# Retention and a two-layer MLP on one core: no key-value products for the last chunk of a batch, and a new order of all work

## The chip, the cores and the metric

The kernel runs on one core of a Trainium2 chip. The time is device microseconds of one execution; the median of several runs is compared. A core has five instruction queues: PE (TensorE, matmuls; its weight loads are listed as PEld), DVE (VectorE), ACT (ScalarE), POOL (GpSimd) and SP (SyncE, DMA issues only). Each works strictly in its own order and waits on semaphores for the others. Matmul results go to PSUM, everything else lies in SBUF.

## The reference, cut to what matters

```
scores = q @ k^T / 8                             # 8 batches, 8 heads, 576 tokens, 64 per head
D[i, j] = gamma_h ** (i - j)  if i >= j else 0
ret = (scores * D) @ v
x = ret as (4608 tokens, 512)                    # heads side by side
h = x @ w_in                                     # 512 -> 2048
g = max(0.01 * h, h)
out = g @ w_out                                  # 2048 -> 512
```

All inputs and the output are float32; the kernel multiplies in float16 and adds up in float32.

## The kernel before, in words

**Retention.** The 576 tokens of a batch are nine chunks of 64. Two chunks in a row, over all eight heads, are a *unit* of 128 tokens: 36 units, u = 0 to 35, chunk numbers 2u and 2u + 1 (j = 0, 1). `CB` is 9, so `(2*u + j) % CB` is the chunk's place in its batch. For each unit q, k and v are loaded in float32 (`ld`u.0, .1, .2 for q, k, v; line 865), cast to float16, q and v with the decay factors (`cq`, `ck`, `cv`, lines 892 to 900: one instruction on VectorE or GpSimd, but eight, one a head, for a scaling on ScalarE), and q and k are turned, by TensorE for units 0 to 7 (`tp`, line 938, and the copy back `yt`, 945) and by a DMA transpose for two units at a time from unit 8 on (`tr`, 921). Then come matmuls of 64x64: scores within the chunk (`sa`, line 973), the key-value product k^T v (`sb`, line 982), masking on VectorE (`mk`, 988), the running state in float32 (`st`, 1031 to 1038) and its float16 copy (`sx`, 1051 and 1054). The output product (line 1096) adds masked scores times v and state times q. These small matmuls come in groups: `oa` (all of a unit's output), `ca` and `ow` (scores with state products, then the unit's own products) and, from unit 13 on, one burst `bu` for everything. The result is copied to xT, turned as layer 1 wants it (`x`u, 1145).

**The MLP.** Tokens go in nine groups of 512, four units each. Layer 1 of groups 0 to 2 is done plainly (`h`group.column.token, line 1201, and the activation `l`, 1208): sixteen matmuls with 128 columns for group 0, eight with 256 for the others. Groups 3 to 8 do layer 1 (`a`, line 1382), and all groups layer 2 (`b`, line 1465), by Winograd's form of Strassen's method: seven half-size products p1 to p7 instead of eight, with sums of weights (`ws`, `wm`), of inputs (`xs`, `m`) and of accumulators, which are copied or added on ScalarE and VectorE (`cA`, `u2`, `k5`, and the four outputs `11`, `12`, `21`, `22`). Four PSUM accumulators (tile acc) are shared by `tp`, `h`, the fillers and the products. Results go out by `so` (line 1293). The weights are loaded by GpSimd's queue: `wi0` to `wi3` are quarters of w_in, `wo0` to `wo3` of w_out.

**What sets the order.** A planner (class `Plan`) gets every job with its engine, an estimated cost, the jobs it comes after, its buffers and a due time. It places the jobs one by one on a model of the five engines and of the DMA queues, the most urgent first, and the program is written in that order. Three tables in `_cfg` steer it: `eng` says which engine does a job where it is not the default, `nudge` shifts the urgency of named jobs, `shift_due` the due times of sets of products. Where the planner sees TensorE waiting early on, it puts in matmuls on a tile of zeros, the fillers (`filler`, line 1574, tile idle):

```
early = t < CFG["fill_tight"]
if t - free < (350 if early else 500) or t > CFG["fill_until"]:
    return None
```

The planner's costs do not run on the chip; only the order, the engines and the number of fillers that follow from them do.

Of the kernel before, what the change touches and what calls it, by code (L numbers as in the profile page):

```python
# [47 lines left out]
class Plan:  # L48
# [72 lines left out]
    def order(self, margin=30, slack=30, filler=None):  # L121
# [57 lines left out]
        while todo:  # L179
# [76 lines left out]
def _cfg():  # L256
# [40 lines left out]
    nudge = {  # L297
        -125060:
            "b1.p2.1 ",
        -12876:  # L300
            "so3.1 ",
        -129001:
            "b1.p4.1 ",
        -135715:
            "b1.21 ",
        -137832:
            "b1.11 ",
        -149466:
            "b2.p4.1 ",
        -1547:  # L310
            "mk25 ",
        -15631:
            "b3.p5.0 ",
        -15982:
            "mk27 ",
        -166028:
            "m3.3.0 ",
        -168918:
            "tp5.1 ",
        -18270:  # L320
            "a7.0.p7.0 ",
        -19132:
            "bu32 ",
        -224663:
            "wm1.1 ",
        -2292:
            "m5.2.1 ",
        -239388:
            "wm0.1 ",
        -23999:  # L330
            "b4.p6.1 ",
        -241662:
            "ws3.1 ",
        -25911:
            "ck33 ",
        -2823:
            "b3.p7.1 ",
        -283444:
            "h1.8.256 ",
        -284183:  # L340
            "b0.11 ",
        -289278:
            "ws3.0 ",
        -291604:
            "h1.10.256 ",
        -292799:
            "h1.4.256 ",
        -292880:
            "h1.14.256 ",
        -293315:  # L350
            "b1.p1.1 ",
        -295060:
            "h2.12.0 ",
        -296205:
            "m0.2.0 ",
        -296904:
            "h1.0.0 ",
        -296915:
            "h1.2.0 ",
        -297398:  # L360
            "wm3.1 ",
        -298104:
            "h1.6.0 ",
        -298106:
            "h1.4.0 ",
        -298370:
            "h1.2.256 ",
        -298539:
            "m0.0.1 ",
        -299439:  # L370
            "tp3.1 ",
        -303300:
            "h2.14.0 ",
        -308278:
            "h1.8.0 ",
        -308311:
            "h1.0.256 ",
        -308822:
            "b1.p1.0 ",
        -309432:  # L380
            "h0.12.256 ",
        -311524:
            "h1.6.256 ",
        -311811:
            "h2.10.0 ",
        -311836:
            "h1.12.256 ",
        -313357:
            "h0.12.384 ",
        -313360:  # L390
            "h0.12.128 ",
        -335793:
            "h0.8.384 ",
        -34182:
            "m5.1.0 ",
        -35130:
            "x32 ",
        -354662:
            "b0.p1.1 ",
        -3566:  # L400
            "h2.8.256 ",
        -357776:
            "h0.4.384 ",
        -367256:
            "b0.p2.1 ",
        -373798:
            "b0.p4.1 ",
        -373977:
            "b0.p2.0 ",
        -37443:  # L410
            "m2.3.1 ",
        -37836:
            "b5.p5.0 ",
        -37837:
            "m5.2.0 ",
        -411099:
            "h0.0.384 ",
        -412537:
            "b1.p2.0 ",
        -42785:  # L420
            "so1.0 ",
        -42873:
            "b6.p6.1 ",
        -43046:
            "b6.cA ",
        -44602:
            "b6.p3.0 ",
        -475499:
            "sb5 ",
        -476800:  # L430
            "tp5.0 ",
        -477521:
            "ow4 ",
        -48742:
            "b7.cA ",
        -5032:
            "bu25 ",
        -5392:
            "st13.1 ",
        -60255:  # L440
            "a8.3.p7.0 ",
        -6102:
            "h2.8.0 ",
        -6129:
            "st22.1 ",
        -6251:
            "h2.10.256 ",
        -6440:
            "st5.1 ",
        -67999:  # L450
            "h2.0.0 ",
        -6861:
            "x13 ",
        -6863:
            "mk15 ",
        -69572:
            "sb6 ",
        -7013:
            "st16.1 ",
        -71217:  # L460
            "ow8 ",
        -741035:
            "h0.8.128 ",
        -7443:
            "bu16 ",
        -78873:
            "sb9 ",
        -79153:
            "ca8 ",
        -7916:  # L470
            "ck31 ",
        -80887:
            "b8.p1.1 ",
        -80940:
            "ow9 ",
        -8500:
            "h2.12.256 ",
        -86291:
            "h2.4.0 ",
        -86992:  # L480
            "ca6 ",
        -87129:
            "ca9 ",
        -88867:
            "h2.6.0 ",
        -91309:
            "ca10 ",
        -9164:
            "h2.14.256 ",
        -93902:  # L490
            "h2.4.256 ",
        -94450:
            "xs4.0 ",
        -94496:
            "cq18 ",
        -949:
            "mk23 ",
        -95343:
            "ck19 ",
        -95691:  # L500
            "sb10 ",
        -97722:
            "h2.6.256 ",
        10483:
            "cq5 ",
        121673:
            "mk3 ",
        132759:
            "b1.u2 ",
        14115:  # L510
            "sx4 ",
        16903:
            "b2.u2 ",
        18328:
            "ck21 ",
        19089:
            "a8.0.p3.0 ",
        20427:
            "cv23 ",
        206971:  # L520
            "h2.2.256 ",
        21595:
            "x28 ",
        221749:
            "h2.2.0 ",
        2247:
            "a5.0.p5.0 ",
        22662:
            "cv9 ",
        24175:  # L530
            "a4.2.p5.0 ",
        24632:
            "x16 ",
        24762:
            "xs4.2 ",
        26177:
            "cq9 ",
        262811:
            "st3.1 ",
        27608:  # L540
            "a5.0.p7.0 ",
        28146:
            "mk18 ",
        28610:
            "a5.0.p3.0 ",
        28749:
            "cq23 ",
        29413:
            "st24.0 ",
        305690:  # L550
            "tr10 ",
        3073:
            "bu27 ",
        30779:
            "a5.0.p2.0 ",
        319187:
            "tr8 ",
        34356:
            "b5.p7.1 ",
        3442:  # L560
            "bu28 ",
        34544:
            "xs5.2 ",
        3603:
            "b4.p5.1 ",
        3689:
            "b1.p6.0 ",
        38799:
            "x29 ",
        4280:  # L570
            "b7.p5.0 ",
        46305:
            "a7.2.p2.0 ",
        4876:
            "b1.p6.1 ",
        54112:
            "b5.p4.0 ",
        5838:
            "b6.p1.1 ",
# [127 lines left out]


CFG = _cfg()


# [972 lines left out]
```

## Time and profile before

| | |
|---|---|
| median of 3 runs | 288.48 us (288.45 to 289.79) |
| the profiled execution | 286.13 us |
| its span, first to last instruction | 284.1 us |
| granted TensorE clock, mean | 0.999 |
| TensorE busy | 274.5 us, 97% |
| VectorE, ScalarE, GpSimd busy | 78%, 64%, 33% |
| HBM read and written | 36.81 MB, 9.44 MB |

The profile is one execution. Its page gives busy times, the span in 40 slices (tenths of busy time, TensorE's clock and the DMA's share), the DMA queues, and the chain of work that ended last. The views of the trace that are used below are groups of instructions by line, the timeline (start, length, engine, line, operation, tiles, count; in brackets the idle time before it and what ended it), and windows (start and end, length, then for each engine busy time and count, TensorE's clock, DMA share and GB/s). "issue" as a releaser means that nothing in the profile accounts for the wait.

### The profile page before, as it was taken

What the parts mean: (1) busy time and instruction counts of PE and PEld (TensorE: products, weight loads), DVE (VectorE), ACT (ScalarE), POOL (GpSimd) and SP (SyncE); (2) the same over time, 40 slices, a digit from 0 to 9 for tenths busy, and PEclk for the clock granted to TensorE, in tenths of its full rate; (3) what the DMA queues carried; (4) which work ended last, traced back from release to release, by engine and by line L of the source; (5) the groups of instructions that cost most, each with busy time, mean ns of one, the idle gap of its engine ahead of it and who ended that gap; (6) DMA issues with size and microseconds to landing.
All of it is one profiled execution on the core that took longest, in us unless ns stands there. A gap on an engine that the chain in (4) does not pass through costs nothing.

```text
span 284.1 us, 10441 instructions
## 1 busy us (share of the span) xinstructions
PE 274.5 (97%) x4530; PEld 231.8 (82%) x4530; DVE 221.9 (78%) x394; ACT 182.2 (64%) x373; POOL 92.9 (33%) x109
## 2 busy tenths in 40 slices
PE   8989899999999999999999999999999999999994
PEld 3668787887788888888888878888888888888883
DVE  3775899865888699898969889889897876955762
ACT  2366576676579598768767766877656755755720
POOL 8888987910122311337324134522100000000000
PEclk9999999999999999999999999999999999999999
DMA  7999999999999999999999999990312002100304
GB/s 158 290 262 237 275 183 284 320 217 228 273 234 194 226 231 272 202 225 240 225 224 212 230 215 229 248 229 0 76 47 105 2 2 76 75 0 3 148 2 148
DMA packets 118797, 50.06 MB, mean 176 GB/s; under 512 B 107488, under 2 KB 112224, under 8 KB 118752
## 3 DMA queue, kind: packets, MB, share of 16 engines
q1 hardware_dynamic: 110368, 35.82, 55.6%
q0 software_dynamic: 7056, 13.11, 19.2%
q8 instruction: 35, 0.57, 0.8%
q10 hardware_dynamic: 1328, 0.47, 0.6%
q14 instruction: 10, 0.08, 0.1%
HBM read 36.81 MB, written 9.44 MB: 163 GB/s over the span
## 4 chain that ended last, share of the span: by engine, by line
PE 82%; DVE 7%; DMA 5%; issue 2%; POOL 2%; ACT 0%; DVEq 0%; POOLq 0%; ACTq 0%
PE acc L1465 38%; PE acc L1382 26%; PE acc L1201 10%; PE ot L1096 4%; DMA w_in<-in_moe_w_in_dram 3%; DMA qkT<-qk 2%; PE sc L982 2%; PE sc L973 2%; POOL t L865 1%; DVE mix L1441 1%; DVE sum L1409 1%; PE acc L938 1%; DVE v L896 1%; DVE s L1037 1%; DVE s L988 1%
## 5 line engine op out<-in xcount | busy, mean ns | idle before, releaser
L1465 PEld LDWEIGHTS <-gt 128*128 128x128 f16 x720 | 69.6, 98 | 8.9 <-ACT gt L1405 0.3
L1465 PE MATMUL acc<-w_out,gt 128*128 128x256 f16 x432 | 54.4, 273 | 0.1
L1201 PE MATMUL acc<-xT,w_in 128*128 128x128 f16 (+1 forms) x512 | 47.1, 246 | 0.5 <-issue 0.5
L1201 PEld LDWEIGHTS <-w_in 128*128 128x128 f16 x512 | 39.1, 98 | 4.4 <-issue 0.7
L1382 PEld LDWEIGHTS <-w_in 128*128 128x128 f16 x384 | 36.8, 98 | 5.5 <-issue 0.8
L1414 ACT ACTIVATE gt<-sum 128x512 f16<-128x512 f32 x48 | 29.8, 629 | 17.8 <-DVE sum L1409 17.7
L1208 ACT ACTIVATE gt<-acc 128x512 f16<-128x512 f32 x48 | 27.8, 594 | 19.9 <-PE acc L1201 19.7
L1405 ACT ACTIVATE gt<-acc 128x512 f16<-128x512 f32 x48 | 28.6, 595 | 14.5 <-PE acc L1382 14.0
L896 POOL TENSOR_TENSOR qk<-t,cs 128x512 f16<-128x512 f32 x19 | 20.6, 1090 | 50.7 <-PE sc L982 22.1
L1465 PE MATMUL acc<-w_mix,gt 128*128 128x256 f16 x288 | 36.4, 273 | 0.0
L1465 PEld LDWEIGHTS <-mix 128*128 128x128 f16 x288 | 27.7, 98 | 4.0 <-DVE mix L1441 0.5
L1382 PEld LDWEIGHTS <-w_sum 128*128 128x128 f16 x288 | 27.6, 98 | 3.9 <-DVE xs L1362 0.4
L1382 PE MATMUL acc<-xs,w_in 128*128 128x256 f16 x192 | 28.8, 273 | 0.7 <-DVE sum L1409 0.7
L1382 PE MATMUL acc<-xs,w_sum 128*128 128x256 f16 x192 | 28.8, 273 | 0.1
L1382 PE MATMUL acc<-xT,w_in 128*128 128x256 f16 x192 | 28.8, 272 | 0.0
L896 POOL TENSOR_TENSOR v<-t,cs 128x512 f16<-128x512 f32 x18 | 20.3, 1127 | 23.7 <-PE ot L1096 19.5
L988 DVE TENSOR_TENSOR s<-sc,cs 128x512 f16<-128x512 f32 x36 | 24.6, 682 | 1.4 <-PE sc L973 1.4
L1335 ACT COPY k<-acc 128x512 f32<-128x512 f32 x27 | 15.9, 591 | 14.2 <-PE acc L1382 7.9
L1409 DVE TENSOR_TENSOR sum<-acc,k 128x512 f32<-128x512 f32 x24 | 16.5, 689 | 7.8 <-ACT k L1335 4.1
L1033 DVE TENSOR_TENSOR s<-sc,s 128x256 f32<-128x256 f32 x40 | 16.7, 418 | 4.1 <-PE sc L982 3.4
L1327 ACT COPY acc<-acc 128x512 f32<-128x512 f32 x30 | 17.4, 579 | 3.1 <-PE acc L1465 1.8
L1096 PE MATMUL ot<-qkT,st 64*64 64x64 f16 x512 | 17.1, 198 | 1.7 <-ACT st L1051 0.5
(68 smaller groups left out, 463.0 us busy)
## 6 DMA issues: line engine op xcount, KB each, us to landing
out_dram<-osb SPq DMA_DIRECT2D x17, 512.0 KB, 4.1
t<-in_k_dram SPq DMA_DIRECT2D x22, 256.0 KB, 4.3
t<-in_q_dram SPq DMA_DIRECT2D x21, 256.0 KB, 4.6
t<-in_v_dram SPq DMA_DIRECT2D x21, 256.0 KB, 4.3
t<-in_v_dram POOLq DMA_DIRECT2D x11, 256.0 KB, 5.5
t<-in_k_dram POOLq DMA_DIRECT2D x10, 256.0 KB, 6.9
t<-in_q_dram POOLq DMA_DIRECT2D x10, 256.0 KB, 6.1
w_in<-in_moe_w_in_dram POOLq DMA_DIRECT2D x8, 256.0 KB, 6.9
```

The lines of the kernel that those rows point to most:

```text
L896: engine[e].tensor_tensor(out=out, in0=t32[u, 2 * x][:], in1=decay(u, x), op=MUL)
L988: landed[u] = nc.vector.tensor_tensor(out=s[:], in0=a[:, :, 0], in1=mask_sb.unsqueeze(1).unsqueeze(1).to_broadcast([P, 2, NP, CH]), op=MUL,)
L1033: nc.vector.tensor_tensor(out=to, in0=x, in1=before[0][:, before[1]], op=ADD)
L1096: i = nc.tensor.matmul(out=ot[half(oo), (j + u) % 2, slot, c, :], lhsT=lhsT, rhs=rhs, start=(first or parted(u)) and (j, oo) not in seen, ...
L1201: nc.tensor.matmul(out=a[:, n, :], lhsT=w_in16[:, c, (f0 + n) * P : (f0 + n + 1) * P], rhs=x[:, c, t0 : t0 + nt], start=(n == 0 and c == 0 ...
L1208: nc.scalar.activation(out=y[:, f0 : f0 + nf, t0 : t0 + nt], in_=a[:], func=mybir.ActivationFunctionType.Lrelu)
L1327: op("cA", ce, lambda: copies[ce](out=B[:], in_=A[:]), [done["1"]], [B], [A], "1", COST[ce, "seed"])
L1382: nc.tensor.matmul(out=r[:, f, :], lhsT=w[:, c, (2 * n + f) * P : (2 * n + f + 1) * P], rhs=rhs[:, c, :], start=fresh and c == 0 and f == ...
L1405: w = op(what, "ACT", lambda: nc.scalar.activation(out=to(), in_=r[:], func=lr), after, [y], [r], m)
L1409: what, "DVE", lambda: nc.vector.tensor_tensor(out=s[:], in0=r[:], in1=plus[:], op=ADD),
L1414: lambda: nc.scalar.activation(out=to(), in_=s[:], func=lr), [j], [y], [s],
L1465: nc.tensor.matmul(out=r[:, tb, :], lhsT=lhs[n]()[:, f, tb * P : (tb + 1) * P], rhs=rhs[n][:, f, :], start=fresh and i == 0 and k == 0, st ...
```

## The change

It does three things.

1. The key-value product is left out for the chunk with place 8, the last of each batch, since its state is not used (the next batch starts from nothing). One such chunk is in each of units 4, 8, 13, 17, 22, 26, 31 and 35. The planner's costs of the jobs follow the number of products.
2. The model of the planner is changed: transfers of the SP and GpSimd queues follow each other instead of sharing, w_out's first quarter has a longer transfer, and fillers are put in from a gap of 300 ns on. The float32 state gets a pool of its own, with the four buffers that it had.
3. `eng`, `nudge` and `shift_due` are new, so that the order of all work on all engines is another, near the old one. The last layer-2 set (b8) keeps its order.

The diff, cut to its core (of the tables `eng` is shown; `nudge` has some 150 new entries of one job each in place of the old ones):

```diff
-                    both = min(j.move, max(0.0, server["POOL"] - at))
-                    server["SP"] = at + j.move + 0.5 * both
-                    server["POOL"] += 0.6 * both
+                    if server["POOL"] > at:
+                        at = server["POOL"]
+                        server["POOL"] += 0.1 * j.move
+                    server["SP"] = at + j.move
                 else:
-                    server["POOL"] = at + j.move + 0.5 * min(j.move, max(0.0, server["SP"] - at))
+                    server["POOL"] = at + j.move + 0.1 * min(j.move, max(0.0, server["SP"] - at))
...
         "ACT":
-            "yt0.0 sx0.0 sx0.1 yt2.1 sx2.1 yt3.1 sx3.0 sx3.1 yt4.0 sx6 sx7 cq8 cq11 cv11 sx10 sx11 cq13 sx12 "
-            "cq16 cv17 sx17 cq18 cv18 cq20 sx21 sx28 ",
+            "sx0.0 yt1.1 cq2 cq3 yt2.1 sx2.1 yt3.1 sx3.0 cv4 cv5 yt4.0 sx5 sx6 cq8 cv10 cv11 sx10 sx11 cv12 "
+            "cq16 cq17 cv17 sx17 cv19 cq20 sx21 sx23 sx28 sx29 ",
         "DVE":
-            "ck0 cq0 cv0 ck1 cv1 x0 yt1.0 sx1.1 sx2.0 ck4 ck5 yt4.1 yt5.0 yt7.1 x7 ck8 x8 x9 x11 cq12 cv12 "
...
+            "cv0 cv1 sx0.1 yt1.0 ck2 ck3 yt2.0 sx2.0 x2 ck4 yt4.1 x4 ck6 cq6 yt6.1 yt7.1 yt7.0 x7 ck8 x8 x9 "
...
         "POOL":
-            "cq2 ck3 sx4 sx5 cv7 cv8 ck9 sx8 cq10 cv10 ck11 sx13 sx14 cq19 sx18 ck23 sx22 ck24 ck25 ck27 cv29 "
-            "cv30 cv32 cv33 cv34 ck35 ",
+            "sx1.0 cv2 sx4 cv8 sx8 ck10 ck11 sx13 sx14 cv16 ck17 cq19 sx18 ck22 ck23 sx22 ck27 ck28 cv30 ck32 "
+            "cv32 cv33 sx33 cv34 ck35 ",
...
+    c_pool = pool("cp", 4)
...
-    BURST = 562
...
+    def states(u):
+        return 4 * (2 - fresh(u, 0) - fresh(u, 1))
...
-        f, h = Buf(a_pool, [P, 2, NP, CH], FP, "s32", turn=u), Buf(a_pool, [P, 2, NP, CH], F16, "st16", turn=u)
+        f, h = Buf(c_pool, [P, 2, NP, CH], FP, "s32", turn=u), Buf(a_pool, [P, 2, NP, CH], F16, "st16", turn=u)
...
         def sb():
             for p in range(NP):
                 for j in range(2):
-                    for g in range(2):
+                    for g in range(2 if live(u, j) else 0):
                         nc.tensor.matmul(
                             out=a[half(g), j, 1, p, :], lhsT=qk16[u][half(j), u % 2, 1, 2 * p + g, :],
                             rhs=v16[u][half(j), 2 * p + g, :], start=True, stop=True, skip_group_check=True,
                         )
...
+            pairs = 32 + lives + states(u - 1) + (states(u - 2) if cross is not None else 0)
+            burst = 31 + 8.3 * pairs
...
-        w_out_job[c] = add(f"wo{c}", "POOL", (770, 770), run, move=2600, due=load_due("POOL"))
+        w_out_job[c] = add(f"wo{c}", "POOL", (770, 770), run, move=3400 if c == 0 else 2600, due=load_due("POOL"))
...
-        if t - free < (350 if early else 500) or t > CFG["fill_until"]:
+        if t - free < (300 if early else 500) or t > CFG["fill_until"]:
```

How the order begins on TensorE, before and after (`fill` stands for one or more fillers):

```
before: fill tp0.1 fill tp0.0 fill sa0 sb0 fill oa0 fill h0.0.0 tp1.1 fill tp1.0 fill sb1 sa1 tp2.1 fill tp2.0
        oa1 sa2 sb2 fill h0.0.128 h0.4.0 oa2 h0.4.128 tp3.0 h0.0.256 h0.4.256 fill h0.8.128 tp3.1 sb3 tp4.1 ...
after:  fill tp0.1 fill tp0.0 sb0 sa0 fill oa0 fill tp1.1 h0.0.0 tp1.0 sb1 tp2.1 fill sa1 fill tp2.0
        oa1 sb2 sa2 fill h0.4.0 h0.0.128 oa2 tp3.1 h0.4.128 sb3 tp3.0 h0.0.256 h0.8.0 sa3 h0.8.128 oa3 ...
```

The first jobs of ScalarE and of GpSimd's queue:

```
ACT before:  yt0.0 sx0.0 sx0.1 l0.0.0 ck2 yt2.1 sx1.0 yt2.0 x1 l0.0.128 sx2.1 l0.4.0 ...
ACT after:   ck0 sx0.0 ck1 x0 yt1.1 l0.0.0 cq2 yt2.1 sx1.1 x1 l0.4.0 cq3 ...
POOL before: ld0.2 wi0 ld1.1 ld1.0 ld1.2 ld2.1 ld2.0 ld2.2 wi1 ld3.1 ld3.0 ld3.2 cq2 wi2 ld4.1 ld4.0 ld4.2 ck3 wi3 ...
POOL after:  ld0.2 wi0 ld1.1 ld1.0 ld1.2 cq0 ld2.1 ld2.0 ld2.2 wi1 ld3.1 ld3.0 ld3.2 sx1.0 cv2 wi2 ld4.1 ld4.0 ld4.2 wi3 ...
```

More of the change, by code (lines that the diff above doesn't have):

```diff
@@ L592, in _cfg @@
-        883:
-            "b4.p4.0 ",
+        -11343:
+            "st15.0 ",
+        -113903:
+            "bu23 ",
+        -12156:
+            "so1.0 ",
+        -1241:
+            "b0.p2.1 ",
+        -13805:
+            "ws2.1 ",
+        -148646:
+            "b1.12 ",
+        -18808:
+            "b4.p2.0 ",
+        -19320:
+            "m5.2.0 ",
+        -2174:
+            "b5.p7.0 ",
+        -225980:
+            "sb9 ",
+        -226700:
+            "ca8 ",
+        -228127:
+            "ow8 ",
@@ new lines, in _cfg @@
+        15478:
+            "b4.p4.0 ",
+        15856:
+            "bu35 ",
+        15857:
+            "cv29 ",
+        16994:
+            "ld6.1 ",
+        18388:
+            "b4.p7.0 ",
+        19227:
+            "b6.p4.1 ",
+        19573:
+            "mk22 ",
+        209881:
+            "st11.0 ",
+        21752:
+            "a6.1.p4.0 ",
+        218671:
+            "tr10 ",
+        22703:
+            "mk26 ",
+        227383:
+            "cv9 ",
+        228859:
+            "sx7 ",
@@ new lines, in _cfg @@
+        23404:
+            "bu26 ",
+        26706:
+            "ld21.0 ",
+        28446:
+            "mk31 ",
+        286869:
+            "st8.0 ",
+        295898:
+            "ck7 ",
+        3329:
+            "a4.2.p1.0 ",
+        3558:
+            "bu19 ",
+        36832:
+            "x28 ",
+        40174:
+            "xs7.3 ",
+        4143:
+            "b7.p5.0 ",
+        46776:
+            "a6.3.cA ",
+        47135:
+            "ld15.0 ",
+        47311:
+            "a5.0.p4.0 ",
@@ L1004, in all_ @@
                 sb()
+            pairs = 32 + lives + states(u - 1) + (states(u - 2) if cross is not None else 0)
+            burst = 31 + 8.3 * pairs
             ja = jb = add(
-                f"bu{u}", "PE", (BURST, BURST + 268), all_,
+                f"bu{u}", "PE", (burst, burst + 268), all_,
                 [turned[u, 0], turned[u, 1], cast[u, 1], cast[u, 2], written.get(u - 2)] + after, [a],
```

645 lines of the change are left out of this document (286 added, 359 removed), and 8 rows, old and new, of the table eng.

## The prediction

> **What bounds the kernel now.** I read the page first, for the busiest engine and the clock.
>
> ```profile
> span 284.1 us, 10441 instructions
> PE 274.5 (97%) x4530; PEld 231.8 (82%) x4530; DVE 221.9 (78%) x394; ACT 182.2 (64%) x373; POOL 92.9 (33%) x109
> PEclk9999999999999999999999999999999999999999
> DMA  7999999999999999999999999990312002100304
> q8 instruction: 35, 0.57, 0.8%
> PE 82%; DVE 7%; DMA 5%; issue 2%; POOL 2%; ACT 0%; DVEq 0%; POOLq 0%; ACTq 0%
> ```
>
> TensorE is busy for 97% of the span at full clock and carries 82% of the chain that ended last. So only three things can shorten the run: less TensorE work, fewer idle fillers (the matmuls on the tile idle), and fewer waits. DMA is full for two thirds of the run. The queue named instruction moves 0.57 MB in 35 packets, 16 KB each; it returns below.
>
> Next, the filler line by stretches, and then all engines by stretches (length, then busy time and count of PE, PEld, DVE, ACT, POOL):
>
> ```profile
> 0.00:17.04 17.04, 10.19 (x31) 3.03 (x31) 1.00 0.99 231
> 17.04:41.16 24.12, 1.37 (x4) 0.30 (x4) 1.00 1.06 238
> 41.16:284.10 242.94, 0.00 (x0) 0.00 (x0) 1.00 0.72 166
> ...
> 17.04:24.11 7.07, 6.42 (x126) 5.85 (x127) 3.41 (x8) 3.86 (x7) 5.16 (x8) 1.00 1.03 244
> 24.11:29.34 5.23, 4.49 (x129) 3.88 (x128) 3.31 (x7) 3.85 (x8) 5.21 (x6) 1.00 1.09 248
> 29.34:35.05 5.71, 5.48 (x126) 4.65 (x127) 5.37 (x8) 3.27 (x7) 5.71 (x8) 1.00 0.95 286
> 35.05:41.16 6.11, 6.05 (x131) 5.40 (x129) 5.41 (x11) 4.88 (x10) 4.96 (x7) 1.00 1.17 179
> 41.16:284.10 242.94, 237.10 (x3802) 204.50 (x3799) 194.51 (x341) 160.19 (x333) 56.93 (x61) 1.00 0.72 166
> ```
>
> All fillers lie ahead of 30 us; 31 of the 34 lie ahead of 17.04, where TensorE waits for the first loads. From 41.16 on, TensorE is busy for 237.1 of 242.9 us, so only short waits are left there.
>
> I chose the edges 17.04, 24.11, 29.34, 35.05 and 41.16 by counting the program's TensorE instructions (matmuls and weight loads): there stand numbers 448, 704, 960, 1216 and 1472, 256 apart, and the windows show 126 to 131 of each kind. The timeline says why:
>
> ```profile
> 17.04 0.39 PE L1574 MATMUL acc<-idle 128*128 128x512 f16 x1 [0.41 <-issue]
> ...
> 22.96 0.61 PE L1201 MATMUL acc<-xT,w_in 128*128 128x128 f16 x8
> 24.11 0.61 PE L1201 MATMUL acc<-xT,w_in 128*128 128x128 f16 x8 [0.54 <-issue]
> 24.55 0.39 PE L938 MATMUL acc<-ident,qk 128*128 128x128 f16 x4
> ...
> 28.45 0.28 PE L982 MATMUL sc<-v,qk 64*64 64x64 f16 x12
> 29.34 0.22 PE L982 MATMUL sc<-v,qk 64*64 64x64 f16 x4 [0.61 <-issue]
> ```
>
> TensorE stops in the middle of a job, after 8 of 16 and after 12 of 16 matmuls, with nothing in the profile that releases it. 256 instructions in a 16 KB packet are 64 bytes each, so I read these stops as waiting for code. While loads fill the DMA engines, a block of 256 instructions took 5.2 to 7.1 us. [...]
>
> **The change, part by part.** *Removed products.* A batch has nine chunks of 64 tokens; the last one's key-value product (line 982) updates a state that nobody reads. Eight matmuls go per batch, 64 in all, with their weight loads. Their spacing, in one late burst:
>
> ```profile
> 211.23 0.32 PE L973 MATMUL sc<-qkT 64*64 64x64 f16 x16
> 211.37 0.31 PE L982 MATMUL sc<-v,qk 64*64 64x64 f16 x16
> 211.61 0.39 PE L1382 MATMUL acc<-xs,w_in 128*128 128x256 f16 x2
> ```
>
> Sixteen start within 0.14 us, 8.8 ns each; the 0.24 us behind the second sixteen holds another 0.10 for the change of shape, which stays. 56 of the 64 lie behind 41 us: 56 x 8.8 ns = 0.5 us gained. Bounds: nothing, if the eight that remain, now all on one half of the rows, take the time of sixteen; and 56 x 27 ns = 1.5 us, half of a 128-column product's 55 ns (8 of them between 24.11 and 24.55), if nothing ran beside them. I take 0.5, since the spacing is that of these very products. [...]
>
> *The new order, to 41 us.* Fillers fall from 34 to 30, and 50 bursts of small matmuls stay 50, so the changes of shape cost the same. The start runs differently:
>
> ```profile
> 5.34 0.94 POOL L865 DMA_DIRECT2D t<-in_v_dram  x1
> 6.21 0.95 POOL L865 DMA_DIRECT2D t<-in_k_dram  x1
> 9.77 0.69 DVE L1145 CAST xT<-ot 128x512 f16<-128x512 f32 x1 [0.48 <-PE ot L1096]
> 10.49 0.75 POOL L1175 DMA_DIRECT2D w_in<-in_moe_w_in_dram  x1 [0.94 <-DMA w_in<-in_moe_w_in_dram]
> 10.54 1.06 PE L1201 MATMUL acc<-xT,w_in 128*128 128x128 f16 x16
> 10.66 0.43 DVE L892 CAST qk<-t 128x512 f16<-128x512 f32 x1 [0.20 <-DMA t<-in_k_dram]
> 13.98 1.08 POOL L896 TENSOR_TENSOR qk<-t,cs 128x512 f16<-128x512 f32 x1
> 49.54 2.01 ACT L900 ACTIVATE qk<-t,cs 128x64 f16<-128x64 f32 x8
> ...
> L892 ACT CAST qk<-t 128x512 f16<-128x512 f32 x14 | 8.5, 617 | 0.8 <-DMA t<-in_k_dram 0.7
> w_in<-in_moe_w_in_dram POOLq DMA_DIRECT2D x8, 256.0 KB, 6.9
> ```
>
> The first query scaling goes to GpSimd, behind the load issue at 5.34, and takes 1.08 there; the loads of unit 2 are asked for 1.1 us later than 6.21. Part of that is free: the second quarter of w_in waited 0.94 in that queue anyway. ScalarE gets the key cast of unit 1 ahead of the copy x0, so x0 and the first layer-1 job wait for a load that comes at 10.66: 10.66 + 0.62 + 0.58 (the scalar copy) = 11.9, against 10.54 now. That 1.3 us is given back where ten fillers (10 x 0.216) stood between this job and 17.04 and seven will. But the query scaling of unit 2 goes to ScalarE (2.01 instead of 1.08): behind the first activation (11.9 + 1.06 + 0.60 = 13.5) it ends near 15.6; for the transposes, their copy and the three bursts that follow I allow 1.5, so 17.1. The next job then needs the second quarter of w_in, asked for at 10.49 and due 6.9 later (the median), at 17.4. So instruction 448 comes at 17.4 instead of 17.04; ends 17.0 and 18.1.
>
> From 448 to 1472 I counted the matmuls of each block, at 55 ns (128 columns), 110 (256), 216 (512), 8.8 (64) and 0.10 per change of shape: 6.1, 4.2, 5.3, 5.8 now, and 5.4, 5.2, 4.9, 4.7 changed, 20.2 against 21.4. The four windows took 24.1. If code comes no faster than now, the new blocks also take 24.1; if it never binds, 20.2 and short waits. The first two windows ended in a code wait, so I keep their 7.07 and 5.23; of the last two, which were nearly all work (11.8), I take 11.3. Sum: 17.4 + 23.6 = 41.0. At 1472 the new order is 0.2 us of work behind (it has done only a part of the first layer-2 job). Against 41.16: 0.0. Ends -2.9 (17.0, and four blocks in 21.0 as below) and +1.2 (18.1 and 24.1).
>
> *The new order, behind 41 us.* The waits now:
>
> ```profile
> 46.78 0.22 PE L1096 MATMUL ot<-qkT,st 64*64 64x64 f16 x2 [0.52 <-ACT st L1051]
> 69.40 0.22 PE L1096 MATMUL ot<-qkT,st 64*64 64x64 f16 x2 [0.29 <-DVE st L1051]
> 75.92 0.25 PE L1096 MATMUL ot<-qkT,st 64*64 64x64 f16 x6 [0.25 <-DMA qkT<-qk]
> 185.60 0.60 PE L1382 MATMUL acc<-xs,w_in 128*128 128x256 f16 x4 [0.70 <-DVE sum L1409]
> 183.08 1.26 DVE L1051 CAST st<-s 128x512 f16<-128x512 f32 x1
> ```
>
> In SP's queue the DMA transpose of units 8 and 9 moves ahead of one load and that of units 10 and 11 ahead of two; the matmuls that read the second have 0.5 us more TensorE work ahead of them: the 0.25 goes. The state cast at 183.08 ahead of the sum that cost 0.70 moves to ScalarE: with 1.26 us less ahead, that wait goes. The first wait halves: between unit 6's key-value product and its next burst stand 3.2 us of TensorE work, not 2.6. Together -1.2. New ones: unit 8's scores and its own output product (ca8, ow8) have one layer-1 job (0.87) between them instead of five jobs, and the masking has to pass on VectorE in that time; ScalarE does thirteen scalings of 2.01 instead of nine, and four accumulators wait for it. I put +0.6 on these: -0.6 together, ends -1.2 (no new ones) and +0.6 (no old one goes). The first store now stands in SP's queue ahead of the values of unit 14; its products come sooner in TensorE's order than now, so it costs nothing, but were they late, the loads of units 14 and 15 and a transpose would queue behind it; likewise the transpose of units 8 and 9 waits for their casts and holds unit 13's loads. The state tiles' own pool keeps four buffers, and the planner's costs alone change otherwise: 0.
>
> **Sum.** 0.0 - 0.5 - 0.6 = -1.1: span 283.0 for 284.1. The profiled execution took 286.13, 2.0 over its span; the median of the runs is 288.48. I subtract from the median: 287.4.
>
> **The rivals.** *Code stops binding* (faster). If a block needs no more than its 5.2 us, or DMA serves code sooner since loads are asked for later, the four blocks take 5.4 + 3 x 5.2 = 21.0 and the early term is 17.4 + 21.0 + 0.2 - 41.16 = -2.6: 284.8; with half of it 286.1. For it: two of four windows were work. Against: the shorter the blocks, the more they meet the limit.
>
> *ScalarE holds the start up* (slower). With 2.01 us scalings and casts ahead of the copies that free accumulators, 448 comes at 18.1, a bank wait of 0.6 (one activation) falls into the first block, and the blocks keep 24.1: 18.1 + 0.6 + 24.1 + 0.2 - 41.16 = +1.8; with the later waits at +0.2 and the products at -0.5: +1.5, 290.0. It decides once 448 is later than 17.9 and the next three blocks show code waits. For it: x0 behind a cast that waits for a load. Against: the seven fillers soak some of it up.
>
> *The removed products were dearer*: 1.5 instead of 0.5, 286.4. *They give nothing*, as the remaining eight take as long: 287.9.
>
> **How the numbers follow.** Forecast 0.48 (own range 286.4 to 288.7), code 0.24, ScalarE 0.18, dearer 0.05, nothing 0.05. A measurement here tells 0.5%, 1.44 us, from no change (the three runs spread by 1.3). Faster than 287.04: code, dearer and a quarter of the forecast, 0.41. Slower than 289.92: 0.17, the rest 0.42. The range reaches from code's full gain to short of ScalarE's: 285.0 to 289.9.
>
> **What would show it.** Right: 30 fillers, all ahead of 20 us; instruction 448 near 17.4 and 1472 near 41; stops named issue in mid-job, 256 instructions apart; no wait at the counterpart of 185.6. Wrong: blocks of 4.7 us without stops (code did not bind), 448 past 18, or new waits over 0.5 us behind 41 us.

## The result and the profile after

The changed kernel took 286.35 us (median of 20 runs, 285.07 to 289.22), the kernel before 288.44 us (20 runs, 286.66 to 290.60): a ratio of 0.994, 95% interval 0.9916 to 0.9964, so 1.0 to 2.4 us less. A second series gave 286.83 us and 0.9931 (0.9897 to 0.9965). Forecast were 287.4 us and a range of 285.0 to 289.9: right, about a microsecond too cautious.

One caution comes ahead of every view. Single executions of one kernel differ by 3 us and more (by 3.9 us over the 20 runs of before, by 4.2 over those of the changed kernel), and a profile shows one of them. The profile that the prediction rests on (286.13 us) was quicker than all 20 runs of its kernel; the one that came with the result took 288.63 us, 2.3 over its median. Subtracted, these two would call the change 2.5 us slower. I read the changed kernel from a repeat that took 286.54 us. Its page:

```profile
span 284.8 us, 10331 instructions
PE 272.9 (96%) x4462; PEld 231.3 (81%) x4462; DVE 221.2 (78%) x392; ACT 187.4 (66%) x401; POOL 94.7 (33%) x111
q8 instruction: 35, 0.57, 0.8%
PE 79%; DMA 8%; DVE 8%; issue 2%; ACT 2%; POOL 1%; DVEq 0%; ACTq 0%; POOLq 0%
```

TensorE issues 68 matmuls less (64 products and four fillers) and is busy for 272.9 us, not 274.5; ScalarE is busy for 187.4 us instead of 182.2, and the other engines within 2 us of before. Next its stretches, cut again at TensorE's instructions 448, 704, 960, 1216 and 1472, and then the filler line alone:

```profile
0.00:17.92 17.92, 14.29 (x221) 7.38 (x222) 8.31 (x18) 7.72 (x19) 15.22 (x23) 1.00 0.98 223
17.92:24.58 6.66, 5.88 (x136) 5.10 (x128) 4.96 (x11) 5.07 (x16) 5.71 (x9) 1.00 1.07 239
24.58:30.46 5.88, 5.56 (x131) 4.90 (x129) 3.04 (x6) 5.15 (x16) 5.60 (x7) 1.00 1.04 231
30.46:36.27 5.81, 5.34 (x131) 4.84 (x128) 4.86 (x10) 5.14 (x15) 5.81 (x8) 1.00 0.95 281
36.27:41.85 5.58, 5.04 (x127) 4.36 (x127) 5.06 (x10) 4.45 (x9) 5.58 (x7) 1.00 1.14 173
41.85:284.76 242.91, 236.78 (x3735) 204.67 (x3732) 194.97 (x340) 159.91 (x332) 56.73 (x61) 1.00 0.73 167
```

```profile
0.00:20.00 20.00, 9.57 (x30) 2.95 (x30) 1.00 0.98 223
20.00:284.76 264.76, 0.00 (x0) 0.00 (x0) 1.00 0.76 172
```

All 30 fillers lie ahead of 20 us. The four blocks took 23.93 us, where 23.6 were forecast. The timeline of the same run shows what the start waits for:

```profile
11.86 0.58 ACT L1153 CAST xT<-ot 128x512 f16<-128x512 f32 x1
12.00 0.40 PE L939 MATMUL acc<-ident,qk 128*128 128x128 f16 x4 [0.68 <-ACT qk L893]
12.48 1.05 PE L1209 MATMUL acc<-xT,w_in 128*128 128x128 f16 x16
14.74 2.02 ACT L901 ACTIVATE qk<-t,cs 128x64 f16<-128x64 f32 x8 [0.57 <-DMA t<-in_q_dram]
18.87 1.95 PE L1209 MATMUL acc<-xT,w_in 128*128 128x128 f16 x32 [0.56 <-DMA w_in<-in_moe_w_in_dram]
25.01 0.72 PE L1209 MATMUL acc<-xT,w_in 128*128 128x128 f16 x10 [0.21 <-issue]
36.67 1.01 PE L1209 MATMUL acc<-xT,w_in 128*128 128x128 f16 x15 [0.18 <-issue]
43.56 0.60 PE L1473 MATMUL acc<-w_out,gt 128*128 128x256 f16 x4 [1.43 <-issue]
```

The first layer-1 job comes at 12.48 (before 10.54) and the next waits for the second quarter of w_in, as forecast. Three jobs stop in their middle, just behind instructions 704, 1216 and 1472. Behind 60 us, the counterpart of the wait at 185.60, and the one wait that is new in every profile of the new order but the last kernel's below:

```profile
111.92 0.60 PE L1390 MATMUL acc<-xs,w_sum 128*128 128x256 f16 x4 [0.64 <-DVE xs L1370]
...
186.41 0.61 PE L1390 MATMUL acc<-xs,w_in 128*128 128x256 f16 x4
```

To see beyond single waits, I took from the matmul records when layer 2 starts its 1st, 65th, 129th, 257th, 385th, 513th and 701st matmul (us):

```
                           1st   65th   129th  257th  385th  513th  701st    end
before, first profile     40.28  57.38  72.88 108.77 141.51 172.07 220.36  284.12
before, repeat            40.38  56.69  73.08 109.87 142.66 173.21 221.49  285.26
before without 6 stores   42.34  58.66  74.41 111.74 144.50 175.06 223.34  287.31
before, cast on ScalarE   41.72  61.21  76.71 112.27 145.00 175.55 223.50  287.3
changed, with the result  43.50  60.12  76.56 112.32 146.51 175.76 223.28  286.86
changed, repeat           41.52  58.91  75.35 110.25 144.43 173.67 221.19  284.76
changed, products kept    42.63  58.01  74.47 109.55 143.71 172.98 220.50  284.12
```

Behind the 257th, stretches of one order agree within 0.2 us (but for the moved cast's 0.34 and, in the seven profiles not listed, the mended wait of the last kernel and two stretches that are 0.6 us longer); ahead of it the marks scatter by up to 4.5 us. So the late part can be read from one profile, best with a second one beside it, and the early part cannot.

From the 257th matmul to the issue of the last store it takes 172.50 and 172.53 us in the two profiles of before, and 171.83 and 171.82 in those of the changed kernel: 0.7 us less. With the products kept it is 171.86, and TensorE then runs the same matmuls there as before (1416 of 256 columns and 1160 of 64, by the records). So this part of the gain comes from the order and is waits alone. From that issue to the end of the span it is 2.86 us before, and 2.69 in the new order and also with the products alone left out; the cause of these 0.17 us was not tried.

### The profile page after: what moved, and what is told of

Its sections match the earlier page's. It is cut to its first block, busy times and chain, and to the rows that moved or that the text cites. A ratio compares the mean times of both kernels' runs of the same rounds, so it can differ in the third digit from the quotient of the medians.

```text
span 286.9 us, 10331 instructions
## 1 busy us (share of the span) xinstructions
PE 273.2 (95%) x4462; PEld 231.5 (81%) x4462; DVE 221.6 (77%) x392; ACT 187.4 (65%) x401; POOL 94.1 (33%) x111
## 4 chain that ended last, share of the span: by engine, by line
PE 75%; DMA 10%; DVE 8%; POOL 3%; issue 2%; ACT 0%; POOLq 0%; DVEq 0%; ACTq 0%
PE acc L1473 35%; PE acc L1390 25%; PE acc L1209 8%; DMA w_in<-in_moe_w_in_dram 5%; PE ot L1104 4%; DMA qkT<-qk 3%; DMA t<-in_v_dram 3%; POOL t L866 2%; DVE mix L1449 2%; PE sc L977 1%; PE sc L986 1%; DVE s L1041 1%; DVE v L897 1%; DVE qk L893 1%; POOL w_in L1183 1%
## 5 line engine op out<-in xcount | busy, mean ns | idle before, releaser
L897 POOL TENSOR_TENSOR qk<-t,cs 128x512 f16<-128x512 f32 x18 | 20.0, 1124 | 38.0 <-PE sc L986 26.4
L1343 ACT COPY k<-acc 128x512 f32<-128x512 f32 x28 | 16.6, 593 | 11.1 <-PE acc L1390 6.3
L1335 ACT COPY acc<-acc 128x512 f32<-128x512 f32 x29 | 16.7, 575 | 7.3 <-PE acc L1473 5.4
L1473 PE MATMUL acc<-w_mix,mix 128*128 128x256 f16 x144 | 18.5, 273 | 0.2 <-DVE w_mix L1257 0.2
```

What stands on the lines that cost most here:

```text
L897: engine[e].tensor_tensor(out=out, in0=t32[u, 2 * x][:], in1=decay(u, x), op=MUL)
L1335: op("cA", ce, lambda: copies[ce](out=B[:], in_=A[:]), [done["1"]], [B], [A], "1", COST[ce, "seed"])
L1343: op("k5", ke, lambda: copies[ke](out=k5[:], in_=C[:]), [done["5"]], [k5], [C], "5")
L1473: nc.tensor.matmul(out=r[:, tb, :], lhsT=lhs[n]()[:, f, tb * P : (tb + 1) * P], rhs=rhs[n][:, f, :], start=fresh and i == 0 and k == 0, st ...
```

## The experiments

**Both halves, and both kernels again.** The products alone, in the order of before, and the new order with the products kept (the same line, the other way round):

```
-                    for g in range(2):
+                    for g in range(2 if live(u, j) else 0):
```

> The changed kernel once more, for a second profile and as the base for its variants on this chip. By every theory the ratio to the kernel before is 0.990 to 0.997. The theories differ in the profile. Loads bind the start (L): instruction 1472 is reached at a time that follows the landing of the first GpSimd-queue load, about 34 us behind it, and the waits between instructions 448 and 1472 name casts (DVE qk, ACT qkT). Code binds the start (C): the waits in that stretch are named issue, in mid-job, 256 instructions apart.

> The kernel before once more, for a second profile. Ratio 1.000 within 0.3%. If the spread of a kernel's times (286.7 to 290.6) is set by when the first loads land (L), then a profile that is 1 us slower shows its first layer-1 job, and instruction 1472, about 1 us later, and the rest as long as before. If the spread arises later, instruction 1472 stays at 41.2 and the rest is longer.

> The kernel before with the products of the last chunk of each batch left out and nothing else changed (same order, same engines, same fillers). Forecast's term: -0.5 us, ratio 0.998. Dearer products: -1.5 us, 0.995. No gain from them: 1.000.

> The changed kernel with those products computed after all, order unchanged: the new order alone. Forecast: +0.5 us on the changed kernel, ratio to the kernel before 0.996 (the order gives 1.6 of the 2.1 us measured). If the products were the whole gain: 1.000. If the products give nothing: 0.994.

Measured: the changed kernel 0.9931 (0.9897 to 0.9965), before again 1.0027 (0.9990 to 1.0065), products alone 0.9961 (0.9929 to 0.9993), order alone 0.9943 (0.9902 to 0.9984). In time, the two halves gave 1.1 us (0.2 to 2.1) and 1.6 us (0.5 to 2.8), more than the whole of 2.0: these intervals cannot divide the gain. The timeline shows that the products are worth little. First the repeat of before, then the kernel with only the products dropped, at the same burst:

```profile
227.24 0.32 PE L982 MATMUL sc<-v,qk 64*64 64x64 f16 x16
227.49 1.05 PE L1465 MATMUL acc<-w_out,mix 128*128 128x256 f16 x8
```

```profile
226.80 0.29 PE L982 MATMUL sc<-v,qk 64*64 64x64 f16 x8
227.03 1.05 PE L1465 MATMUL acc<-w_out,mix 128*128 128x256 f16 x8
```

Sixteen products take 0.25 us to the next job, eight take 0.23. By the records these eight start at 0, 3, 32, 35, 63, 67, 95 and 98 ns: in pairs, 32 ns apart, all eight on the same row half. A burst gains 20 ns, not 8 x 8.8; eight bursts gain 0.16 us. From the 257th matmul of layer 2 to the issue of the last store, with four of the eight bursts, the kernel without the products takes 172.62 us, against 172.50 and 172.53: no gain is seen there.

Of the theories on the start neither holds alone. The repeat of before was 1.0 us slower, but its first layer-1 job came at 10.34 (10.54) and instruction 1472 at 41.27 (41.16), so the first loads did not make the difference; it came behind, where TensorE waited 1.15 us for a transpose instead of 0.25. In the repeat of the changed kernel the waits between instructions 448 and 1472 have names of both kinds, issue as well as loads and copies.

**Moving the code stops.** The early fillers cut into four of 128 columns: about the same time by the usual spacing (4 x 55.5 ns for 216), but 84 TensorE instructions more in the changed kernel and 66 in the one before, so the 256-instruction blocks end in other jobs.

```
+        cuts = 4 if free < WARM else 1
-            for _ in range(n):
-                nc.tensor.matmul(out=a[:, 0, :], lhsT=idle[:, 0:P], rhs=idle, start=True, stop=True)
+            for i in range(n * cuts):
+                cs_ = slice(i % cuts * TOK // cuts, (i % cuts + 1) * TOK // cuts)
+                nc.tensor.matmul(out=a[:, 0, cs_], lhsT=idle[:, 0:P], rhs=idle[:, cs_], start=True, stop=True)
```

> The changed kernel; each of the 14 fillers ahead of 7 us is cut into four of 128 columns (the same TensorE time, 84 instructions more). Nothing behind them changes, but every later job stands 84 instructions further on. Code theory (C): stops come at a count of 256 instructions, so the 1.43 us stop inside the first layer-2 job (instruction 1472 in the changed kernel) leaves that job, and stops named issue stand 84 instructions earlier in the order of jobs; that job starts 0.5 to 1.4 us sooner, ratio to the kernel before 0.988 to 0.992. If the stops belong to the job (its loads or buffers), they stay in it and the ratio stays at 0.993.

> The kernel before with its 11 fillers ahead of 7 us cut into four each (66 instructions more). Code theory (C): the stops at 23.35 (after 8 of 16 matmuls of a layer-1 job) and at 28.53 (after 12 of 16 small products) leave these places; new ones may stand 66 instructions earlier. Time: 0 to -1 us, ratio 0.997 to 1.000. If the stops belong to the jobs: same places, 1.000.

Measured: 0.9955 (0.9923 to 0.9987) for the changed kernel, 1.0034 (1.0003 to 1.0065) for the one before. The stops moved with the count. In the shifted kernel before, each row right behind instruction 704, 960 or 1216 (23.27, 29.68, 35.39 us by the records):

```profile
23.88 1.46 PE L1201 MATMUL acc<-xT,w_in 128*128 128x128 f16 x23 [0.39 <-issue]
30.50 0.23 PE L1096 MATMUL ot<-s,v 64*64 64x64 f16 x5 [0.62 <-issue]
36.72 0.25 PE L1096 MATMUL ot<-qkT,st 64*64 64x64 f16 x4 [1.14 <-issue]
```

In the first profile of before, code packets of 16 KB landed at 22.74 and 27.77 us by the DMA records, and TensorE went on 1.4 and 1.6 us later (24.11 and 29.34). In the shifted changed kernel each packet had landed 2.7 to 4.6 us before its block was reached, and from 15 to 50 us no stop named issue of 0.1 us or more is left. Nothing was won: the waits had other names, and layer 2 began at 43.41 (41.52 and 43.50 in the two profiles of the changed kernel). The shifted kernel before was 0.1 to 1.9 us slower, which neither theory had; why, was not tried.

```profile
20.21 1.95 PE L1209 MATMUL acc<-xT,w_in 128*128 128x128 f16 x32 [0.49 <-DMA w_in<-in_moe_w_in_dram]
40.29 0.25 PE L1104 MATMUL ot<-qkT,st 64*64 64x64 f16 x6 [0.49 <-ACT qkT L946]
41.74 1.05 PE L1209 MATMUL acc<-xT,w_in 128*128 128x128 f16 x16 [0.73 <-DVE qkT L946]
```

So code makes the stops here, but it does not set the pace of the start: where its stops went, loads (0.49 us) and copies (0.49 and 0.73) stopped TensorE instead. That rests on one profile and on times that agree within their intervals.

**Late transposes: stores taken out.** Theory T said that a typical run of before loses its time to DMA transposes that land late. Both kernels without the first six stores of 512 KB (the outputs of the first three of the nine token groups are not written):

```
-            nc.sync.dma_start(out=out[r0 : r0 + HT, :].rearrange("(t p) d -> p t d", p=P), in_=o[:])
+            if g > 2:
+                nc.sync.dma_start(out=out[r0 : r0 + HT, :].rearrange("(t p) d -> p t d", p=P), in_=o[:])
```

> The kernel before without the stores of the first three layer-2 groups (six transfers of 512 KB between 72 and 138 us are left out, so their part of the output is missing). Late transposes theory (T): in a typical execution TensorE waits for DMA transposes that land just before their bursts, more than in the profile first read; with 3 MB less ahead of them the waits go: -1.2 to -2.5 us, ratio 0.991 to 0.996, and the spread narrows. Without such waits: 0.999 to 1.000.

> The changed kernel without the same stores. T with the new order: its bursts stand later and its transposes earlier, so there is less to gain: 0 to -0.8 us on the changed kernel, ratio to the kernel before 0.990 to 0.993. If the new order's gain has nothing to do with transposes, it gains as much as the kernel before does: 0.985 to 0.989.

Measured: before 1.0012 (0.9981 to 1.0043), changed 0.9907 (0.9871 to 0.9944), both as with the stores. But the transpose was no earlier, so T was not yet tried. The timeline of before without the stores, on TensorE and SP:

```profile
42.34 1.05 PE L1466 MATMUL acc<-w_out,gt 128*128 128x256 f16 x8 [1.53 <-DMA w_out<-in_moe_w_out_dram]
...
72.23 5.94 SPq L921 DMA_TRANSPOSE qkT<-qk  x2
...
78.88 0.25 PE L1096 MATMUL ot<-qkT,st 64*64 64x64 f16 x6 [1.68 <-DMA qkT<-qk]
```

**Late transposes: moved in SP's queue.** In this and the next three kernels a kernel's order is written out as a list of job names that the planner must follow, so nothing else moves (in the last of them the planner puts in two more fillers, 32 for 30).

```
-... ld13.0 ... tr8 ...    ld15.1 ld15.0 ld15.2 tr10
+... tr8 ld13.0 ...        ld15.1 tr10 ld15.0 ld15.2
```

> The kernel before with its whole order kept, but for SP's queue: the DMA transpose of units 8 and 9 stands ahead of one load (the queries of unit 13) and that of units 10 and 11 ahead of two (queries and values of unit 15), as in the changed kernel. Theory T (late transposes): the casts of unit 11 were done at 62.0 in the profile without the first stores, yet the transpose was issued at 72.2 and landed at 78.83, and TensorE waited 1.68 us for it; in the three profiles of the kernel before and of that one this wait was 0.25, 1.15 and 1.68, so a typical run loses about 1 us there. Then no wait over 0.2 us at the first matmul of unit 10, and a ratio near 0.997 (-0.9 us). Rival U: the two loads behind it come as much later, their casts or the next transpose wait in its place, and the ratio is 1.000.

Measured: 1.0008 (0.9972 to 1.0044). In its profile the transpose is issued 1.6 to 4.2 us sooner than in the first profile of before, its repeat and the one without stores (69.71, 70.49, 72.23), landed at 73.30, 2.7 us ahead of its reader, and TensorE does not wait:

```profile
68.07 3.24 SPq L921 DMA_TRANSPOSE qkT<-qk  x1
...
76.05 0.26 PE L1096 MATMUL ot<-qkT,st 64*64 64x64 f16 x8
```

The wait went and the time stayed. The 0.997 of T lies just outside the interval, so T falls as the source of the whole gain; a smaller one is not excluded: the interval reaches 0.8 us, and outside its span this kernel spends 2.11 us where before spends 1.92 (medians; cause not tried).

**One cast.** Unit 29's state cast on ScalarE, in the order of before:

```
-            "cq16 cv17 sx17 cq18 cv18 cq20 sx21 sx28 ",
+            "cq16 cv17 sx17 cq18 cv18 cq20 sx21 sx28 sx29 ",
```

> The kernel before with its whole order kept, but for one engine: the cast of unit 29's state goes from VectorE (1.26 us at 183.08) to ScalarE, at the same place of the order. If this cast was what made the 0.70 us wait at 185.60, the wait goes, the 48.3 us from the 513th to the 701st matmul of layer 2 become 47.6, and the ratio is near 0.9975 (-0.7 us). If VectorE's other work there (two sums and a mix) sets it, 0.3 to 0.7 us of the wait stay, and the ratio is 0.999 to 1.000.

Measured: 0.9979 (0.9948 to 1.0010). From the 513th to the 701st matmul it took 47.95 us, not 48.28: 0.34 of the 0.70 gained. The timelines of VectorE and TensorE:

```profile
186.56 1.53 DVE L1441 TENSOR_TENSOR mix<-gt 128x1024 f16<-128x1024 f16 x1
188.01 0.68 DVE L1409 TENSOR_TENSOR sum<-acc,k 128x512 f32<-128x512 f32 x1
...
188.74 0.60 PE L1382 MATMUL acc<-xs,w_in 128*128 128x256 f16 x4 [0.24 <-DVE sum L1409]
```

The mix stands ahead of the sum in the kernel before too, but there it is short:

```profile
184.26 0.68 DVE L1441 TENSOR_TENSOR mix<-gt 128x1024 f16<-128x1024 f16 x1
```

The cast had held VectorE for 1.18 us (183.08 to 184.26), and the mix, now earlier, took 0.85 of them back: at 186.56 GpSimd is still busy with its own scaling of values (186.05 to 187.54), while in before that scaling is over at 184.06. In all 14 profiles, behind 60 us, such an instruction of VectorE (two inputs, 128x1024, float16) took 0.67 to 0.69 us in the 901 cases in which GpSimd computed nothing as it began; in the 44 in which a GpSimd scaling was running, it ended 0.54 us or more after that scaling. In the new order the same stretch takes 47.51 us: the mix takes 1.53 there too, but VectorE's scaling ahead of it 0.76 instead of 1.27 us.

This profile holds something else. It waited long for w_out, and here are its stretches around that wait (the column behind POOL's is TensorE's clock):

```profile
41.72 1.05 PE L1465 MATMUL acc<-w_out,gt 128*128 128x256 f16 x8 [2.15 <-DMA w_out<-in_moe_w_out_dram]
```

```profile
39.50:41.72 2.22, 0.08 (x2) 0.00 (x1) 2.20 (x4) 1.03 (x3) 2.22 (x4) 1.00 1.15 184
41.72:44.00 2.28, 2.28 (x16) 1.78 (x17) 0.84 (x1) 0.00 (x0) 2.28 (x3) 0.72 1.24 209
44.00:46.00 2.00, 2.00 (x10) 1.14 (x8) 0.00 (x0) 0.60 (x1) 1.44 (x2) 0.50 1.24 205
46.00:48.00 2.00, 2.00 (x33) 1.77 (x33) 1.49 (x4) 1.21 (x3) 0.69 (x1) 0.96 1.20 272
```

After 2.15 us of waiting the clock fell to half: 0.28 x 2.28 + 0.50 x 2.00 + 0.04 x 2.00 = 1.7 us more. The next kernel shows the same after 2.21 us, with a clock of 0.65 from 42.76 to 45.00 and of 0.54 from 45.00 to 47.00: 0.35 x 2.24 + 0.46 x 2.00 = 1.7 us. The waits of 1.53 and 1.68 us above cost no clock: it is 1.00 in the profile without the stores from 40 to 50 and from 60 to 100 us.

**Three parts together in the old order.** The two transposes, the cast, and the products left out (the three edits shown).

> The kernel before with three things and otherwise its own order: the two transposes earlier in SP's queue, unit 29's cast on ScalarE, and the 64 products left out whose result nobody reads. If the gains add: -0.9, -0.7 and -0.5 make -2.1 us, a ratio of 0.993, as much as the whole change, and the start of the kernel before, about a microsecond quicker in the profiles, could bring it to 0.990. If they hide one another, or the new order's gain comes from elsewhere: 0.996 to 0.998.

Measured: 0.9962 (0.9931 to 0.9993), 287.21 us. The gains did not add up to the 0.993 of the change, though the interval just reaches it.

**The start and one wait mended in the new order.** The edits, by engine and by place in the order:

```
 ACT:  -... cq2 ...           +... sx1.0 ... sx16 ...
 DVE:  -... sx16 ...          +cq0 ... cv2 ...
 POOL: -sx1.0 cv2 (and cq0)   +cq2
 order: cq0 ahead of yt0.1; x0 ahead of ck1; cv2 behind mk1; xs3.1 ahead of xs3.2
```

> The changed kernel with its order kept, but for two places. Start: the queries of unit 0 on VectorE and those of unit 2 on GpSimd as in the kernel before, the first state cast of unit 1 on ScalarE and the values of unit 2 on VectorE, and the copy x0 ahead of unit 1's key cast instead of behind it. At 112 us: unit 16's state cast on ScalarE and the second input sum of group 3 ahead of the third, since all profiles of the new order show a wait of 0.4 to 0.6 us for that sum. Theory S (engine placement cost the start what the prediction said, and nothing else binds there): the first layer-1 job comes at 11.2 instead of 12.5, the second quarter of w_in is asked for a microsecond earlier, instruction 448 comes near 17.0 instead of 17.9, the first layer-2 job about a microsecond earlier, and the wait at 112 goes: -1.5 us against the changed kernel, a ratio to the kernel before of 0.988. Rival L (loads and code bind behind 18 us): the quicker start ends in waits for w_in, for w_out (which lands near 41.5) or in stops named issue, and only the wait at 112 is gained: 0.991 to 0.992.

Measured: 0.9897 (0.9863 to 0.9931), median 286.41: the lowest ratio of all, some 0.3% below the changed kernel's, in another series and with overlapping intervals, so that it beats the changed kernel is not shown. Theory S (0.988) and rival L (0.991 to 0.992) both lie inside the interval; the profile decides between them. Its timeline:

```profile
9.78 0.58 ACT L1153 CAST xT<-ot 128x512 f16<-128x512 f32 x1 [0.96 <-PE ot L1104]
11.81 0.40 PE L939 MATMUL acc<-ident,qk 128*128 128x128 f16 x4 [0.66 <-ACT qk L893]
12.04 1.06 PE L1209 MATMUL acc<-xT,w_in 128*128 128x128 f16 x16
19.22 0.94 PE L1209 MATMUL acc<-xT,w_in 128*128 128x128 f16 x14 [0.20 <-DMA w_in<-in_moe_w_in_dram]
42.50 1.05 PE L1473 MATMUL acc<-w_out,gt 128*128 128x256 f16 x8 [0.23 <-DMA w_out<-in_moe_w_out_dram]
113.41 0.60 PE L1390 MATMUL acc<-xs,w_sum 128*128 128x256 f16 x4
```

The wait at 112 is gone, and from the 257th to the 385th matmul it takes 33.39 us instead of 34.18. One part of it is again GpSimd: in the repeat of the changed kernel a mix ahead of the input sums begins 0.05 us after a GpSimd scaling has begun and takes 1.54 us (108.46); here it begins 0.16 us ahead of that scaling and takes 0.69 (110.54). It is only a part: in the shifted changed kernel that mix took 0.68 and 0.41 us of the wait stayed. The start gained nothing. x0 came 2.1 us sooner, but the first layer-1 job stands behind unit 1's turn in TensorE's order, and that waits for the key cast, whose load lands at 11.1. The second quarter of w_in was asked for 0.55 us sooner and landed at 19.1, not at 18.7. Rival L is what the profile shows.

## Why the prediction was right, point by point

**Removed products** (-0.5, bounds 0 and -1.5): wrong in size: -0.16 by the shown 20 ns a burst, and nothing to be seen behind the 257th matmul. The step that failed is the choice of the spacing of sixteen for the eight that go; its lower bound named the reason, that the eight left stand on one half of the rows. Timed, the products alone gave 0.2 to 2.1 us, so time alone would have passed 0.5 as right.

**The order to instruction 1472** (0.0, ends -2.9 and +1.2): 41.85 in the repeat, against 41.16 and 41.27 in the two profiles of before: +0.6 or +0.7, inside the ends. 448 came at 17.92 instead of 17.4 (18.51 in the profile that came with the result). The mis-sized terms are at the front: the first layer-1 job at 12.48 rather than 11.9, since the key load ahead of x0 landed at 11.31, not 10.66 (x0 ended at 12.44; unit 1's turn, which TensorE also has ahead of that job, was over by then), and unit 2's queries done at 16.76 rather than 15.6, since their load came at 14.7. The next job waited for w_in as said. The blocks were right to 0.3 us. The reason given for them was only half right: the stops are code, and moved with the count, but with the stops gone the start took no less time. The rival that code stops binding is thus wrong as a gain. Two small readings of this part are off without bearing on it: 30 of the 34 fillers start ahead of 17.04 (the one at 17.04 is counted in both windows), and the end of -2.9 is -3.0 by its own terms.

**The later waits** (-0.6): right in sum behind the 257th matmul, not in pieces, and open ahead of it. From the table, less the matmuls' own time in each stretch (their usual spacing: 55.5, 109.2 and 216 ns by width, 8.3 for the small ones), the repeat of the changed kernel against the two profiles of before: 1st to 65th 2.69 us of waits against 1.93 and 1.14; 65th to 129th 1.20 against 1.40 and 2.29; 129th to 257th 2.48 against 2.47 and 3.37; 257th to 385th 2.33 against 1.69 and 1.75; 385th to 513th 1.01 against 1.39 and 1.38; 513th to 701st 2.06 against 2.77 and 2.76; from there to the end 5.12 against 5.24 and 5.25. Behind the 257th that is +0.6 - 0.4 - 0.7 - 0.1 = -0.6. Ahead of it the pieces cannot be read from one profile: the first holds the code stop of 1.43 and is 0.8 to 1.6 us worse, the next two are 0.2 to 1.1 and 0.0 to 0.9 us better. The wait at 185.60 went as forecast, though the cast alone was worth half of it. The new cost came, near the +0.6 that was put on it, but at 112 us behind VectorE's input sums, not behind unit 8's masking or ScalarE's scalings. The wait for the transpose at 75.92 does not go for good: 0.34 us of it is in the new order with the products kept, and 0.67 and 1.17 us are in the shifted changed kernel and in the last one. The profile that came with the result waits for another transpose:

```profile
96.55 0.32 PE L977 MATMUL sc<-qkT 64*64 64x64 f16 x16 [0.95 <-DMA qkT<-qk]
```

**The sum.** The terms that were read do not add up to the timed -1.7 to -2.0 us (interval -1.0 to -3.0): the repeat's span of 284.76 lies between the 284.12 and 285.26 of the two profiles of before, which were both quicker than the median. What agrees between profiles is the part behind the 257th matmul, with 0.7 and 0.17 us less. The time outside the span fell by 0.14 us (median of the runs, 1.92 to 1.78; cause not tried). That leaves 0.7 to 1.0 us, which by this subtraction lie ahead of the 257th matmul, where the forecast's terms nearly cancel. So that the total of -1.1 came within a microsecond is in part luck: it had 0.3 too much for the products and, by the subtraction, missed a gain in the early part.

One place could hold that gain. In the eight profiles of the old order, edited or not, layer 2's first job waits for w_out five times, by 0.64, 1.00, 1.53, 2.15 and 2.21 us, the last two with half a clock behind them; in the six of the new order once, by 0.23. The next row is the repeat of before:

```profile
40.38 1.05 PE L1465 MATMUL acc<-w_out,gt 128*128 128x256 f16 x8 [1.00 <-DMA w_out<-in_moe_w_out_dram]
```

The new order puts other work there. That this is where the missing microsecond went is argued, not shown: the new order's own start is later by about as much, no kernel with only that job moved was run, and the starts scatter by more than the gain. The half clock by itself is not the answer. By the granted clock of the single runs, 24 of 112 executions of before and 5 of 32 of the changed kernel had 0.994 or less (3.4 us at one half, twice the 1.7 us above, make 0.994), and without them the medians still lie 1.9 us apart, 288.14 and 286.23. The rest stays open.

**The rivals.** *ScalarE holds the start up* had the place right and decided too little: 448 came at 17.92, right at its point of 17.9, yet the rest made up for it. *They give nothing* (287.9) was nearly true of the products. What would show it wrong did show in part, 448 past 18 in one profile, and behind 41 us a code stop of 1.43 and a wait of 0.64, without the time getting worse.

## What to carry to other kernels

When single executions scatter by more than the change is worth, take a profile near the median before subtracting anything, and read only those stretches that agree between repeats. Removing half of a burst of small matmuls saved little here, 20 ns of 0.25 us, where the rest stood on one row half: look at how the survivors start, not at the spacing of the full burst. This start, in which the DMA engines were full (a share of 0.95 to 1.14 up to 41.85 us), passed from one wait to the next (code, weights, copies), so removing one of them moved no time; a late wait behind one VectorE job could be mended by moving two jobs (33.39 us instead of 34.18 for that stretch). Before counting on the time that a moved job sets free on VectorE, look at what GpSimd does in that time: here 0.85 of 1.18 us were lost again.

## What the runs showed of the hardware

Behind TensorE waits of 2.15 and 2.21 us (with unit 29's cast on ScalarE, and with the three parts together) the granted clock stood at one half for about 3.4 us, twice the 1.7 us lost; behind waits of 1.53 and 1.68 us (before without the stores) it stayed at 1.00. If it fell in one step, then 1.0 and 0.7 us after TensorE had resumed, as worked out from the clocks of 0.72 and 0.65 in the first 2.28 and 2.24 us. A VectorE instruction that took 0.68 us in before took 1.53 where it began with 0.98 us of a GpSimd scaling left to run. Eight 64x64 products on one row half started in pairs every 32 ns, where the products were left out; sixteen on both halves started within 0.14 us, 8.8 ns each. The page of before has 35 code packets, 0.57 MB, for 9060 matmuls and weight loads; stops stood right behind TensorE's instructions 704 and 960 (0.54 and 0.61 us) and, with 66 instructions put in ahead, stood behind the same counts in other jobs (0.39 and 0.62 us).
